# A longer hand-written order for the opening of a fused attention and feed-forward kernel

## Chip, cores and metric

The kernel runs on one core of a Trainium2 chip. The metric is device time in microseconds: the median of a few executions of the whole program. Executions taken for the trace are listed apart, and all views below are of one such execution.

## What is computed

Attention of 4 batches, 8 heads, 768 positions and 64 dimensions, in which each query sees the keys less than 16 positions away and, besides, 24 summary keys (the maximum over blocks of 32 keys) with summary values (the mean over the same blocks). Its output, 3072 rows of 512, goes through a feed-forward layer of 2048 hidden units with a soft gate:

```
k_sum = k.reshape(B, H, nb, block, D).max(axis=3)
v_sum = v.reshape(B, H, nb, block, D).mean(axis=3)
a = softmax([where(|i-j| < 16, scale * q k^T, -1e9), scale * q k_sum^T + log(32)])
x = a @ [v, v_sum]                      # -> (3072, 512)
h = x @ w_in                            # (512, 2048)
g = where(h >= 1, h, where(h <= -1, 0, (h + 1) ** 2 / 4))
out = g @ w_out                         # (2048, 512)
```

All data are float32; the two weight matrices reach the chip as 64-bit words and are turned into float32 there.

## The kernel before

**Tiling.** The rows are cut into 8 chunks of 384 (`c` = 0 to 7, two chunks a batch). A chunk's attention runs in 4 head couples (`p` = 0 to 3, two heads each). The hidden units are cut into 16 blocks of 128 (`f` = 0 to f, written in hexadecimal). The weights come in 16 tiles (`i` = 0 to f): tile i with i even holds blocks i and i+1 of `w_in`, tile i with i odd holds blocks i-1 and i of `w_out`.

**Steps.** Every piece of work is a step with a letter and its indices. Those that matter here, with their engine:

- SyncE (its queue issues all transfers): `r` raw keys of a couple (line 209), `y` raw values (228), `k`, `q`, `v` windows (215, 220, 235), `w` a weight tile (116, 119), `m` the mask (452), `g` the identity (465), `o` a result (448).
- TensorE: `S` scores (300), `T` transposes (344), `Z` transpose of the summary values (273), `A` values (358), `F` one of four pieces of a hidden block, three matmuls (395), `B` a hidden block into the output, nine matmuls (436).
- VectorE: `R` key maxima (248), `Y` value sums (256), `M` mask and row maxima (311, 315), `D` reciprocals (335), `c` six pieces a weight tile (150, 153, 165), `I` the gate's minimum (413), `L` the low part of x (381).
- ScalarE: `E` exponentials (326), `i` guard of the sums (331), `a`, `b` the first two conversions of a weight tile (132, 142), `G`, `H`, `J` of the gate (401, 407, 418), `V` the means (279), `P` and `X` evictions (351, 376), `U` an output tile out of the accumulators (444, the middle one on VectorE at 442).
- GpSimd: `K` key windows of the first chunk, `C` summary keys into the key tile (251), `N` normalisation (339), `W` summary values into the value tile (284), `d` and `e` the two halves of a weight tile (174, 186), `O` the low part of the gate (423).

So a head couple runs S, M, E, i, D, N, T, P, A, X, L, and needs C before S, and Z, V, W before A. A hidden block runs F, G, H, I, J, O, B. A weight tile runs w, a and b, c, d, e.

**What sets the order.** The string `OPENING` lists steps; `do(OPENING)` issues them under `tc.manual_schedule()`, in which every engine takes its instructions in the order of the list. It holds all of chunk 0, all weights, and the attention of chunk 1 with its first two hidden blocks. Behind it, from line 525 on, loops issue the rest under a manual order for TensorE alone; for the other engines a planner sorts the instructions, and it may also put one of these ahead of an instruction of the list. A step that stands in `done` is not issued twice. In the loop, hidden blocks come in pairs; at f = 2, 6, 10, 14 `turn` transposes a couple of the next chunk and issues the loads and sums of the couple after it (`r`, `k`, `q`, `R`, `C`), and at f = 0, 4, 8, 12 `meet` issues `A`, `X`, `L` of that couple and then `S` of the next one.

**Buffers.** The tag `w` of the pool `stage` has three buffers (`W_BUFS = 3`). They hold the raw keys `r` and values `y` of later batches, a weight tile between `c` and `e`, and the output tiles from `U` to the end of their store `o`. `ps` has six PSUM buffers, the hidden blocks two of their own.

**Small lists.** `P_DVE` and `X_DVE` name evictions that VectorE makes in place of ScalarE; `HI_POOL` names the weight tiles whose `d` GpSimd makes, the others being ScalarE's.

Of the kernel before, what the change touches and what calls it, by code (L numbers as in the profile page):

```python
# [38 lines left out]
LAG = 2  # L39
E_BUFS = 2  # L40
OPENING = """
r00 R00 K00 C00 q00 r01 R01 S00 m h M00 E001 E000 K01 g C01 q01 r03 i00 w0 y00 r02 K03 S01 b0 a0 R03 q02 M01 D00
N001 T001 P001 Y00 R02 Z00 E011 E010 N000 C03 T000 P000 i01 K02 C02 S02 c01 c00 c02 c04 c03 V00 w4 v00 b4 W00 q03
D01 y02 a4 M02 c05 N011 N010 d0 e0 E021 E020 y01 w2 c40 Y02 y03 v01 k10 v02 w1 A00 T010 P010 Y01 c42 c44 T011 P011
i02 X00 D02 S03 L00 M03 q10 N020 N021 b2 n Z01 V01 Z02 a2 V02 F010 T021 T020 Y03 Z03 W01 C10 c20 E030 F000 V03 W02
E031 c41 c21 A01 i03 c22 c23 v03 D03 N031 P021 P020 X01 k11 k12 v10 c24 A02 S10 N030 q12 q11 c43 c25 L01 T031 t d2
b1 T030 F001 w3 a1 X02 P030 P031 W03 M10 E101 A03 F011 X03 C11 e2 L02 c10 c45 C12 E100 i10 L03 F002 F012 F003 F013
w6 d4 G00 G01 H00 c11 c12 S11 D10 N101 S12 w8 w5 c14 c13 N100 I00 H01 T101 W10 w7 c15 I01 J00 F020 q13 T100 d1 k13
v12 wa wb w9 wc q20 F021 b3 P100 F030 O00 P101 M11 k20 r20 M12 a3 c31 F022 e1 F031 c30 c33 c32 c34 c35 F023 A10 wd
we F032 B00 F033 J01 O01 a6 G02 E120 H02 b6 I02 G03 H03 B01 e4 c60 b5 a5 J02 I03 J03 F040 c62 F050 d3 e3 F041 F051  # L50
X10 O02 b8 c61 c63 c64 F042 c50 c65 F052 c52 c51 c54 a8 F043 B02 F053 G04 a7 O03 c53 c55 H04 d6 e6 G05 H05 B03 d5 e5
I04 c80 I05 F060 b7 c81 c82 J05 L10 c83 c84 J04 aa E121 c70 c85 c72 c71 ba F070 i12 a9 c74 c73 c75 D12 F061 F071 O04
F062 F072 F063 B04 O05 d8 e8 G06 F073 G07 H06 I06 H07 B05 I07 ca0 ca2 ca1 ca4 ca3 ca5 F080 F090 F081 d7 N121 N120
T120 F091 P120 J06 F082 F092 J07 b9 e7 O06 F083 F093 T121 W12 da E110 E111 i11 G08 O07 ac H08 c90 c92 P121 c94 c91
I08 B06 A12 ea B07 c93 bc D11 X12 G09 H09 c95 d9 J08 O08 e9 bb F0a0 cc1 ab I09 cc0 L12 cc2 F0b0 cc3 J09 cc4 cc5 cb0
cb1 F0a1 ae cb3 cb2 cb4 F0b1 F0a2 F0b2 F0a3 F0b3 B08 O09 N111 T111 B09 dc G0a H0a G0b H0b be ec C13 I0a cb5 J0a P111
I0b v13 ce0 ce1 ce2 ce4 ce3 ce5 db N110 J0b v11 wf F0d0 ad bd F0c0 O0a F0d1 bf F0c1 F0d2 eb S13 F0c2 F0d3 F0c3 R20
O0b B0a M13 G0d T110 G0c H0d I0d cd0 C20 de ee W13 B0b H0c E130 E131 i13 F0f0 cd1 I0c J0c cd2 cd3 cd4 cd5 F0e0 F0f1
F0e1 af D13 cf0 cf1 cf2 F0f2 F0e2 F0f3 F0e3 O0c W11 N131 P110 dd cf4 cf3 A11 T131 J0d G0e H0e ed B0c O0d N130 cf5
I0e F110 G0f J0e H0f T130 X11 B0d P131 P130 I0f O0e F100 L11 df ef A13 J0f F111 F101 B0e F102 O0f B0f F112 X13 L13  # L60
F103 F113 U01 U02 U00 o02 o00 o01
"""
FIRST = [[("k", 2), ("q", 2)], [("k", 3), ("q", 3)], [("kraw", 1), ("vraw", 1)], [("kraw", 2), ("vraw", 2)],
         [("kraw", 3), ("vraw", 3)], [("v", 2), ("v", 3)], [("q", 0), ("q", 1)]]
K_COPY = "gggg"
H_DVE = "".split()
P_DVE = "110 120 121 131".split()
X_DVE = "11 13".split()
X_POOL = "".split()
F_DVE = "".split()  # L70
A_POOL = "".split()
HALF = "".split()
MASK_PE = "".split()
LATE = []
HI_POOL = [0, 1, 2, 3, 4, 5, 6, 8, 9, 10, 14, 15]


@with_exitstack
def fused_kernel(ctx: ExitStack, tc: tile.TileContext, q2, kT, kwin, vT, vwin, w_in, w_out, mask, ident, out):
# [28 lines left out]
    def room(i, what, shape, dtype):  # L108

        return wpool.tile(shape, dtype, tag=f"w{i}", name=f"{what}{i}")  # L110
# [60 lines left out]
    def convert_high(i):  # L171
        halves[i] = room(i, "halves", [P, 2, 2 * DM], F32R)
        if i in HI_POOL:
            nc.gpsimd.tensor_copy(out=halves[i][:, 0], in_=converting[i].bitcast(F32))
# [171 lines left out]
    def turned(c, p, j):  # L346
        pts[c, p, j] = att.tile([P, T], F32, tag=f"pt{j}", name=f"pt{c}_{p}_{j}", bufs=1)
        if f"{c}{p}{j}" in P_DVE:
            nc.vector.tensor_copy(out=pts[c, p, j][:KA], in_=t_pss[c, p, j][:KA, :T])
# [18 lines left out]
    def high(c, p):  # L368
        hi = xpool.tile([P, T], F32R, tag=f"xhi{p}", name=f"xhi{c}_{p}")
        lo = xpool.tile([P, T], F32R, tag=f"xlo{p}", name=f"xlo{c}_{p}")  # L370
        if f"{c}{p}" in X_POOL:
            nc.gpsimd.tensor_copy(out=hi, in_=fulls[c, p])
        elif f"{c}{p}" in X_DVE:
            nc.vector.tensor_copy(out=hi, in_=o_pss[c, p][:, :T])
# [233 lines left out]
```

## Time and profile before

| | us |
|---|---|
| median of 3 executions | 643.02 (642.08 to 643.59) |
| the profiled execution, whole | 644.87 |
| its span, first to last instruction | 643.1 |
| TensorE busy in it | 620.2 |
| ScalarE busy | 356.4 |
| GpSimd busy | 267.2 |
| VectorE busy | 245.2 |

The views are read like this: a timeline row has the start, the length, the engine, the line and operation, the tile written and the tiles read, the shape, and the number of like instructions put together; in brackets stands how long the engine had been idle before it and what released it. A row of the stages has the busy time of each engine in a stretch, the mean clock granted to TensorE, and the share and rate of the transfers. PEld is TensorE's weight load, SPq is SyncE's queue.

### The profile page before, as it was taken

The page shows a single profiled execution, that of the slowest core. Times are in us where ns is not written, and L with a number is a line of the kernel's source. Part 1 is how long each engine was busy: PE and PEld are TensorE (multiplying, and loading weights), DVE is VectorE, ACT ScalarE, POOL GpSimd, SP SyncE. Part 2 cuts the span into 40 slices and gives each one's busy share as a digit, 9 for nine tenths or more (in the row PEclk, how much of TensorE's full clock was granted, in tenths as well). Part 3 has the DMA queues.
Part 4 walks back from the last instruction along what each step waited for, and adds up shares of the span by engine and source line. Part 5 has one row for each costly group of instructions (what it writes and reads, how often), then busy time and mean ns, then how long its engine had stood idle before and what let it go on. Part 6 is the DMA issues. An engine that isn't in the chain of part 4 may idle for free.

```text
span 643.1 us, 11595 instructions
## 1 busy us (share of the span) xinstructions
PE 620.2 (96%) x4426; PEld 551.0 (86%) x4426; DVE 245.2 (38%) x465; ACT 356.4 (55%) x953; POOL 267.2 (42%) x307
## 2 busy tenths in 40 slices
PE   3699999899999999999999999999999999999997
PEld 2488888698888998898898898899889889889996
DVE  6989996542224322242122522142222312221111
ACT  4889994645545544654555554564454455443332
POOL 4689998334234333233334332334432333322221
PEclk9889999999999999999999999999999999999999
DMA  9999721632215222250123521052222200000001
GB/s 334 412 358 414 272 97 50 226 116 73 73 53 194 71 73 73 73 194 27 48 73 131 187 73 48 26 195 73 73 73 71 74 29 19 2 23 28 1 1 49
DMA packets 28167, 72.04 MB, mean 112 GB/s; under 512 B 2800, under 2 KB 3056, under 8 KB 28112
## 3 DMA queue, kind: packets, MB, share of 16 engines
q1 hardware_dynamic: 28112, 71.30, 31.5%
q8 instruction: 35, 0.57, 0.4%
q14 instruction: 20, 0.16, 0.1%
HBM read 65.00 MB, written 6.29 MB: 111 GB/s over the span
## 4 chain that ended last, share of the span: by engine, by line
PE 93%; DMA 4%; ACT 1%; issue 1%; POOL 1%; DVE 0%; SPq 0%; POOLq 0%; DVEq 0%
PE h L395 41%; PE acc L436 41%; PE o_ps L358 4%; PE s_ps L300 3%; PE t_ps L344 3%; DMA v<-in_vwin 2%; DMA first<-in_q 1%; DMA first<-in_kT 1%; ACT e L326 0%; POOL e L339 0%; ACT o L444 0%; ACT t L401 0%; POOL glo L423 0%; DVE e L311 0%; POOL v L284 0%
## 5 line engine op out<-in xcount | busy, mean ns | idle before, releaser
L395 PE MATMUL h<-xhi,halves 128*128 128x384 f32 x1024 | 277.8, 340 | 1.0 <-DVE t L413 1.0
L436 PE MATMUL acc<-halves,ghi 128*128 128x512 f32 x768 | 237.4, 390 | 0.0
L423 POOL TENSOR_TENSOR glo<-t,ghi 128x384 fp32r<-128x384 f32 x128 | 129.3, 1013 | 197.4 <-PE acc L436 184.5
L395 PEld LDWEIGHTS h<-xhi,halves 128*128 128x128 f32 x1024 | 186.2, 188 | 7.9 <-issue 4.0
L395 PE MATMUL h<-xlo,halves 128*128 128x384 f32 x512 | 172.2, 336 | 0.0
L436 PEld LDWEIGHTS acc<-halves,ghi 128*128 128x128 f32 x768 | 144.3, 188 | 28.3
L413 DVE SCALAR_TENSOR_TENSOR t<-h,t 128x384 f32<-128x384 f32 x128 | 71.0, 556 | 214.7 <-ACT t L407 212.9
L436 PE MATMUL acc<-halves,glo 128*128 128x512 f32 x384 | 152.6, 397 | 0.0
L401 ACT ACTIVATE t<-h,small 128x384 f32<-128x384 f32 x128 | 73.2, 573 | 90.9 <-PE h L395 89.2
L326 ACT ACTIVATE e<-e,den 128x120 f32<-128x120 f32 x192 | 73.3, 384 | 56.3 <-DVE den L315 56.3
L395 PEld LDWEIGHTS h<-xlo,halves 128*128 128x128 f32 x512 | 96.4, 188 | 1.8 <-DVE xlo L381 0.2
L418 ACT CAST ghi<-t 128x384 fp32r<-128x384 f32 x128 | 65.0, 510 | 54.5 <-DVE t L413 35.9
L436 PEld LDWEIGHTS acc<-halves,glo 128*128 128x128 f32 x384 | 72.2, 188 | 12.9 <-POOL glo L423 0.2
L407 ACT ACTIVATE t<-t 128x384 f32<-128x384 f32 x128 | 66.5, 524 | 2.2
L339 POOL TENSOR_TENSOR e<-e,den 128x360 f32<-128x360 f32 x64 | 49.2, 788 | 44.0 <-DVE den L335 43.6
L284 POOL COPY v<-mean 24x768 f32<-24x768 f32 x30 | 24.6, 821 | 84.4 <-DMA v<-in_vwin 45.6
L381 DVE TENSOR_TENSOR xlo<-o_ps,xhi 128x384 fp32r<-128x384 f32 x32 | 17.7, 554 | 79.0 <-ACT xhi L376 78.8
L376 ACT CAST xhi<-o_ps 128x384 fp32r<-128x384 f32 x30 | 14.3, 477 | 57.2 <-PE o_ps L358 57.2
L186 POOL TENSOR_TENSOR halves<-w,halves 128x1024 fp32r<-128x1024 f32 x16 | 38.6, 2412 | 0.6
L358 PEld LDWEIGHTS o_ps<-pt,v 120*64 120x64 f32 x720 | 24.6, 143 | 13.6 <-issue 10.6
L326 ACT ACTIVATION_READ_ACCUMULATOR e<-e,den 128x1 f32 x192 | 36.0, 188 | 0.0
L344 PE MATMUL t_ps<-ident_sb,e 128*120 128x128 f32 x192 | 29.3, 286 | 4.2 <-POOL e L339 4.2
(61 smaller groups left out, 404.6 us busy)
## 6 DMA issues: line engine op xcount, KB each, us to landing
v<-in_vwin SPq DMA_DIRECT2D x29, 384.0 KB, 3.3
q<-in_q SPq DMA_DIRECT2D x28, 384.0 KB, 4.3
k<-in_kwin SPq DMA_DIRECT2D x28, 360.0 KB, 5.0
raw<-in_w_in SPq DMA_DIRECT2D x8, 1024.0 KB, 11.3
raw<-in_w_out SPq DMA_DIRECT2D x8, 1024.0 KB, 13.3
out<-o SPq DMA_DIRECT2D x24, 256.0 KB, 2.1
kraw<-in_kT SPq DMA_DIRECT2D x13, 384.0 KB, 3.6
vraw<-in_vT SPq DMA_DIRECT2D x13, 384.0 KB, 3.9
```

The source lines that it names most:

```text
L186: nc.gpsimd.tensor_tensor(out=lo, in0=converting[i].bitcast(F32), in1=hi.bitcast(F32), op=ALU.subtract)
L326: nc.scalar.activation(out=es[c, p, j][:, t, :], in_=s[:, t, :], func=AF.Exp, bias=nm[:, t:t + 1], scale=scale, accum_out=den[:, t:t + 1])
L339: nc.gpsimd.tensor_tensor(out=e, in0=e, in1=den.unsqueeze(2).broadcast_to([P, NT, KA]), op=ALU.mult)
L344: nc.tensor.transpose(t_pss[c, p, j][:KA, t * P:(t + 1) * P], es[c, p, j][:, t, :], ident_sb)
L358: nc.tensor.matmul(o_pss[c, p][j * D:(j + 1) * D, cols], v_ts[c, p][:KA, blk, j * D:(j + 1) * D], pts[c, p, j][:KA, cols], start=True, sto ...
L395: nc.tensor.matmul(hs[c, f][:, :T], w[:, k], x, start=(k == 0 and n == 0), stop=(k == NK - 1 and n == len(products) - 1))
L401: nc.scalar.activation(out=ts[c, f], in_=hs[c, f][:, :T], func=AF.Relu, bias=ones_half, scale=0.5)
L407: nc.scalar.square(out=ts[c, f], in_=ts[c, f])
L413: nc.vector.scalar_tensor_tensor(out=g, in0=hs[c, f][:, :T], scalar=1.0, in1=ts[c, f], op0=ALU.max, op1=ALU.min)
L418: nc.scalar.copy(out=hi, in_=ts[c, f])
L423: nc.gpsimd.tensor_tensor(out=lo, in0=ts[c, f], in1=hi.bitcast(F32), op=ALU.subtract)
L436: nc.tensor.matmul(acc[c][i], a[:, rows], w, start=(f == 0 and n == 0), stop=(f == NF - 1 and n == len(products) - 1))
```

## The change

The list of the opening is replaced. The new one has 592 steps, the old one 544; no step of the old list is missing. The 48 that are added were issued by the loops before: hidden blocks 2 and 3 of chunk 1 (`F120` to `F133`, their `G`, `H`, `I`, `J`, `O`), `B10` and `B11`, and the couple (2, 0) from `y20`, `v20` and `S20` to `T200`, `T201`, `P200`, `P201`, with `Z20`, `V20`, `W20`. The order of nearly all other steps is new as well. The mask goes ahead of all loads; the scores of three couples come before the first transposes; weight tile 0 is loaded after nine loads of keys, queries and values, where it was loaded after five; tile 4 is converted after 2 and 1, where it was second. The three small lists are exchanged too: `P_DVE` 120, 121, 131 go, 111, 130, 200 come; `X_DVE` 13 goes, 03 comes; `HI_POOL` 10 and 14 go, 11 and 12 come.

The diff, with the first and the last lines of the two lists:

```diff
 OPENING = """
-r00 R00 K00 C00 q00 r01 R01 S00 m h M00 E001 E000 K01 g C01 q01 r03 i00 w0 y00 r02 K03 S01 b0 a0 R03 q02 M01 D00
-N001 T001 P001 Y00 R02 Z00 E011 E010 N000 C03 T000 P000 i01 K02 C02 S02 c01 c00 c02 c04 c03 V00 w4 v00 b4 W00 q03
-D01 y02 a4 M02 c05 N011 N010 d0 e0 E021 E020 y01 w2 c40 Y02 y03 v01 k10 v02 w1 A00 T010 P010 Y01 c42 c44 T011 P011
...
-I0e F110 G0f J0e H0f T130 X11 B0d P131 P130 I0f O0e F100 L11 df ef A13 J0f F111 F101 B0e F102 O0f B0f F112 X13 L13
-F103 F113 U01 U02 U00 o02 o00 o01
+m r00 R00 h K00 C00 q00 r01 R01 S00 M00 q01 K01 C01 E001 E000 i00 y00 r02 q02 r03 S01 y02 g R02 M01 K02 C02 w0 E010
+E011 y01 D00 Y00 v00 K03 N001 Y02 R03 S02 N000 Z00 T001 V00 i01 Z02 V02 P001 b0 D01 C03 N011 q03 N010 T000 M02 v01
+w2 a0 Y01 P000 E021 T010 c00 c02 Z01 V01 W00 c04 A00 T011 W01 c01 E020 c03 X00 L00 c05 i02 D02 n P010 P011 S03 A01
+d0 N020 T020 y03 k10 q10 N021 w1 C10 T021 M03 Y03 S10 a2 b2 t X01 e0 c20 L01 E030 E031 P020 i03 P021 c22 c21 c24 D03
+N030 Z03 v02 F010 W02 M10 b1 a1 V03 E100 c23 k12 v03 N031 T030 c10 c11 c25 A02 T031 P030 W03 F011 F000 c13 P031 C12
+X02 L02 c12 E101 d2 e2 A03 w4 q12 w3 q13 F001 F002 k13 a4 i10 w6 w5 X03 w7 b4 c14 L03 D10 w8 c15 c40 c41 c42 I01 I00
...
+F0f3 cd1 B0b af I0e cd2 cd4 v11 F0c0 cd3 L12 E130 G0f i13 H0f T111 I0f cd5 C20 F0c1 N110 J0e T110 O0e W11 F0c2 F0d0
+D13 P111 bf F0c3 P110 cf0 cf2 dd G0c H0c I0c J0c F0d1 A11 X11 F0d2 F110 L11 F0d3 ed N131 T131 F111 O0c N130 W13 cf1
+G0d H0d I0d P131 B0c cf3 cf4 cf5 F100 F112 T130 P130 F101 J0d S20 A13 X13 L13 y20 M20 Y20 O0d F102 B0d F103 df ef
+B0e F113 G10 H10 J0f O0f I10 F130 G11 v20 B0f J10 H11 E201 I11 J11 Z20 F120 V20 F131 F121 E200 O10 F132 F122 F133
+B10 G13 i20 U02 D20 W20 O11 F123 N201 B11 H13 I13 J13 O13 N200 G12 H12 U01 I12 J12 T200 T201 U00 P201 O12 o00 o02
+P200 o01
 """
...
-P_DVE = "110 120 121 131".split()
-X_DVE = "11 13".split()
+P_DVE = "110 111 130 200".split()
+X_DVE = "03 11".split()
...
-HI_POOL = [0, 1, 2, 3, 4, 5, 6, 8, 9, 10, 14, 15]
+HI_POOL = [0, 1, 2, 3, 4, 5, 6, 8, 9, 11, 12, 15]
```

Nothing else differs; what is computed is the same. Behind the new list TensorE's next steps are `A20`, then `S21`, then hidden block 4 of chunk 1; behind the old one they were `S20`, hidden blocks 2 and 3, `Z20`, `T200`, `T201`, `B10`, `B11`, `A20`, `S21`.

More of the change, by code (lines that the diff above doesn't have):

```diff
@@ L41 @@
 OPENING = """
-r00 R00 K00 C00 q00 r01 R01 S00 m h M00 E001 E000 K01 g C01 q01 r03 i00 w0 y00 r02 K03 S01 b0 a0 R03 q02 M01 D00
-N001 T001 P001 Y00 R02 Z00 E011 E010 N000 C03 T000 P000 i01 K02 C02 S02 c01 c00 c02 c04 c03 V00 w4 v00 b4 W00 q03
-D01 y02 a4 M02 c05 N011 N010 d0 e0 E021 E020 y01 w2 c40 Y02 y03 v01 k10 v02 w1 A00 T010 P010 Y01 c42 c44 T011 P011
-i02 X00 D02 S03 L00 M03 q10 N020 N021 b2 n Z01 V01 Z02 a2 V02 F010 T021 T020 Y03 Z03 W01 C10 c20 E030 F000 V03 W02
-E031 c41 c21 A01 i03 c22 c23 v03 D03 N031 P021 P020 X01 k11 k12 v10 c24 A02 S10 N030 q12 q11 c43 c25 L01 T031 t d2
@@ L47 @@
[L47 to L56, printed above, removed]
@@ L57 @@
-I0b v13 ce0 ce1 ce2 ce4 ce3 ce5 db N110 J0b v11 wf F0d0 ad bd F0c0 O0a F0d1 bf F0c1 F0d2 eb S13 F0c2 F0d3 F0c3 R20
-O0b B0a M13 G0d T110 G0c H0d I0d cd0 C20 de ee W13 B0b H0c E130 E131 i13 F0f0 cd1 I0c J0c cd2 cd3 cd4 cd5 F0e0 F0f1
-F0e1 af D13 cf0 cf1 cf2 F0f2 F0e2 F0f3 F0e3 O0c W11 N131 P110 dd cf4 cf3 A11 T131 J0d G0e H0e ed B0c O0d N130 cf5
-I0e F110 G0f J0e H0f T130 X11 B0d P131 P130 I0f O0e F100 L11 df ef A13 J0f F111 F101 B0e F102 O0f B0f F112 X13 L13
-F103 F113 U01 U02 U00 o02 o00 o01
+m r00 R00 h K00 C00 q00 r01 R01 S00 M00 q01 K01 C01 E001 E000 i00 y00 r02 q02 r03 S01 y02 g R02 M01 K02 C02 w0 E010
@@ new lines @@
+E011 y01 D00 Y00 v00 K03 N001 Y02 R03 S02 N000 Z00 T001 V00 i01 Z02 V02 P001 b0 D01 C03 N011 q03 N010 T000 M02 v01
+w2 a0 Y01 P000 E021 T010 c00 c02 Z01 V01 W00 c04 A00 T011 W01 c01 E020 c03 X00 L00 c05 i02 D02 n P010 P011 S03 A01
+d0 N020 T020 y03 k10 q10 N021 w1 C10 T021 M03 Y03 S10 a2 b2 t X01 e0 c20 L01 E030 E031 P020 i03 P021 c22 c21 c24 D03
+N030 Z03 v02 F010 W02 M10 b1 a1 V03 E100 c23 k12 v03 N031 T030 c10 c11 c25 A02 T031 P030 W03 F011 F000 c13 P031 C12
+X02 L02 c12 E101 d2 e2 A03 w4 q12 w3 q13 F001 F002 k13 a4 i10 w6 w5 X03 w7 b4 c14 L03 D10 w8 c15 c40 F012 F013 G01
@@ new lines @@
+c41 c42 F003 G00 v10 H01 I01 H00 I00 S12 c44 N101 N100 T101 T100 b3 d1 e1 c43 M12 J00 P101 J01 a3 O00 c30 c45 O01
+C13 F020 d4 e4 F030 F021 F031 F022 F032 F023 wa P100 we b6 G02 k11 w9 k20 B00 F033 H02 c32 B01 c31 c34 c33 a6 I02
+G03 H03 c35 I03 J02 b5 a5 F050 d3 O02 e3 F040 E120 J03 O03 c61 c60 c63 F051 F041 c62 c50 c64 E121 c52 c65 F052 F042
+F053 F043 G04 G05 H05 H04 c51 c54 c53 B02 S13 I05 i12 b8 a8 I04 d6 e6 c55 J04 B03 M13 J05 F070 c80 c81 c82 F060 c83
+b7 a7 c84 F071 F061 F072 d5 D12 v13 wd q20 c70 c85 O04 e5 F062 F073 ae aa O05 W10 d8 F063 G06 G07 c71 H07 ba B04 e8
@@ new lines @@
+A10 X10 H06 c72 c73 C11 c74 I07 c75 I06 a9 J06 B05 d7 F090 ca0 ca1 wf be ca2 b9 wb F080 ca3 ca4 L10 q11 ca5 F091 J07
+F081 c90 F092 F082 N120 O06 F093 F083 e7 c91 da B06 wc r20 O07 c92 G09 G08 H09 H08 ad N121 T121 B07 ea c93 c94 c95
+v12 I08 P121 d9 J08 O08 e9 I09 ce0 ce1 ce2 F0b0 J09 bb F0a0 F0b1 ab F0a1 ce3 ce4 ce5 T120 cb0 cb1 bd P120 F0a2 cb2
+cb3 cb4 cb5 F0b2 F0a3 F0b3 B08 W12 O09 de G0b G0a H0b H0a A12 ee I0a I0b S11 ac M11 J0b bc cc0 cc1 cc2 cc3 cc4 cc5
+E131 R20 B09 F0e0 F0f0 E111 F0e1 db O0b eb F0f1 F0e2 J0a O0a dc X12 F0f2 E110 i11 D11 N111 F0e3 cd0 ec G0e H0e B0a
```

## The prediction, made before the result was known

> **What bounds the kernel now.** I read the page's totals first, then the stages, then the timeline where a stage shows TensorE idle.
>
> ```profile
> span 643.1 us, 11595 instructions
> PE 620.2 (96%) x4426; PEld 551.0 (86%) x4426; DVE 245.2 (38%) x465; ACT 356.4 (55%) x953; POOL 267.2 (42%) x307
> ```
>
> ```profile
> 28.00:30.00 2.00, 0.57 (x11) 0.68 1.02 404
> ...
> 36.00:38.00 2.00, 1.82 (x29) 1.00 0.96 265
> ...
> 112.00:128.00 16.00, 13.12 (x87) 10.94 (x86) 7.82 (x14) 9.79 (x29) 4.62 (x6) 1.00 0.64 219
> ```
>
> TensorE is busy for 620.2 of 643.1 us. The change takes no work off it, so only its 22.9 idle us can move, and the time in which its granted clock is low. In the stages (stretch, TensorE busy, clock; the last row has all engines) the clock has fallen at 28 to 30 us and is 1.00 again from 36; after that, 112 to 128 stands out with 13.12 us busy of 16. Two places, then: the first 33 us, and the passage from the list to the loops. The opening, TensorE alone:
>
> ```profile
> 5.07 1.48 PE L300 MATMUL s_ps<-k,first 64*64 64x120 f32 x24 [5.07 <-POOL k L251]
> ...
> 13.47 0.89 PE L344 MATMUL t_ps<-ident_sb,e 128*120 128x128 f32 x3 [3.09 <-POOL e L339]
> ...
> 19.00 1.55 PE L358 MATMUL o_ps<-pt,v 120*64 120x64 f32 x24 [1.91 <-POOL v L284]
> ...
> 31.98 1.55 PE L358 MATMUL o_ps<-pt,first 120*64 120x64 f32 x24 [1.00 <-issue]
> ```
>
> The first scores, the first transposes and the first values wait for GpSimd. The last such gap ends at 31.98; from there TensorE has work up to the second place:
>
> ```profile
> 118.79 0.44 PE L395 MATMUL h<-xhi,halves 128*128 128x384 f32 x1 [1.03 <-DVE t L413]
> ...
> 124.40 0.27 PE L273 MATMUL vs_ps<-ident_sb,vsum 128*24 128x128 f32 x1 [1.05 <-DVE den L335]
> ...
> 125.28 0.54 PE L344 MATMUL t_ps<-ident_sb,e 128*120 128x128 f32 x3 [0.60 <-POOL e L339]
> ...
> 126.02 0.54 PE L344 MATMUL t_ps<-ident_sb,e 128*120 128x128 f32 x3 [0.20 <-POOL e L339]
> ...
> 130.61 0.92 PE L358 MATMUL o_ps<-pt,v 120*64 120x64 f32 x24
> 131.46 0.85 PE L300 MATMUL s_ps<-k,q 64*64 64x120 f32 x24
> ```
>
> Four gaps, 1.03 + 1.05 + 0.60 + 0.20 = 2.88 us: `S20` came just before, and between it and `T200` stood hidden blocks 2 and 3 alone, too little to cover mask, exponentials and normalisation. Here 130.61 is `A20` and 131.46 is `S21`. Everything that TensorE did before 131.46 it also does before `S21` in the new order, and behind `S21` both orders are alike, so **the change is worth the shift of `S21`**, and a lower clock behind it if TensorE has stood still.
>
> **First term: the gap at 118 to 126 goes, -2.88 us.** The new list has `S20` ahead of `A13`, three blocks `B0d` to `B0f`, hidden blocks 2 and 3 and `B10`, `B11`. The two blocks `B10`, `B11` alone took from 126.56 (126.02 + 0.54) to 130.61, 2.03 us each; five such blocks and the hidden ones more than cover what stood between `S20` and `T200`.
>
> **Second term: the opening.** VectorE and GpSimd turn the weights while TensorE waits, so I follow them to a place that both lists reach with the same work: the last piece of weight tile 3.
>
> ```profile
> 6.64 0.95 DVE L248 TENSOR_REDUCE ksum<-first 128x24 f32<-128x768 f32 x1 [2.00 <-DMA first<-in_kT]
> ...
> 27.52 1.88 DVE L150 TENSOR_SCALAR c<-raw 128x512 int32<-128x512 int32 x3 [0.47 <-ACT raw L132]
> ...
> 30.96 0.19 DVE L335 RECIPROCAL den<-den 128x6 f32<-128x6 f32 x1 [0.38 <-ACT den L331]
> ...
> 35.03 0.97 DVE L311 SCALAR_TENSOR_TENSOR e<-s_ps,mask_sb 128x360 f32<-128x360 f32 x2 [1.65 <-POOL first L284]
> 35.92 0.95 DVE L315 TENSOR_REDUCE den<-e 128x3 f32<-128x360 f32 x2
> ...
> 49.48 1.29 DVE L165 CUSTOM_DVE_ANT_0 w<-raw,c 128x1024 uint16<-128x1024 uint16 x2
> ```
>
> ```profile
> 21.62 2.37 POOL L186 TENSOR_TENSOR halves<-w,halves 128x1024 fp32r<-128x1024 f32 x1
> ...
> 50.84 1.04 POOL L174 CAST halves<-w 128x1024 fp32r<-128x1024 f32 x1
> 51.96 2.43 POOL L186 TENSOR_TENSOR halves<-w,halves 128x1024 fp32r<-128x1024 f32 x1
> ```
>
> ```profile
> L423 POOL TENSOR_TENSOR glo<-t,ghi 128x384 fp32r<-128x384 f32 x128 | 129.3, 1013 | 197.4 <-PE acc L436 184.5
> ```
>
> VectorE ended that piece at 50.77 (49.48 + 1.29). Up to it the new list has one mask step less (35.03 to 36.87, 1.84 us) and one eviction and one gate minimum more (the minimum takes 556 ns, the row of L413 below, and I take the eviction, of the same shape, as long): -0.73. The waits of 0.47, 0.38 and 1.65 us should go, since tile 2's conversions stand earlier on ScalarE and `S10` earlier on TensorE: -2.50. The wait of 2.00 us for the second raw keys stays and grows by about 0.4, my estimate for the mask that is now issued ahead of them. So the piece ends at 50.77 - 0.73 - 2.50 + 0.4 = 47.9. On GpSimd `d3` (1.04), `O02` (1.01) and `e3` (2.43, the row at 51.96, which ended at 54.39) follow: 52.4, 2.0 us earlier, while the piece on VectorE is 2.9 earlier. These tiles feed TensorE just in time, so **I take -2.4 us**, between the two. Bounds: 0, if TensorE runs dry at the start. Tile 0's second half ended at 23.99 (21.62 + 2.37), and in the new order it comes later: its load is behind four more loads, its pieces behind three more steps of VectorE, its split behind five more of GpSimd. The other end is -3.2, 0.73 and 2.50 with the mask for nothing.
>
> **Third term: what `S21` waits for now.** It needs summary keys, `C21`, these need `R21`, and this the raw keys `r21`, which lie in one of three buffers with the weight tiles and the output tiles.
>
> ```profile
> 102.74 7.15 SPq L235 DMA_DIRECT2D v<-in_vwin  x2
> ...
> 116.07 1.32 SPq L448 DMA_DIRECT2D out<-o  x3
> ...
> 118.83 0.37 SPq L209 DMA_DIRECT2D kraw<-in_kT  x1
> ...
> 124.28 0.33 SPq L209 DMA_DIRECT2D kraw<-in_kT  x1
> ...
> 127.34 0.95 DVE L248 TENSOR_REDUCE ksum<-kraw 128x24 f32<-128x768 f32 x1 [0.34 <-DMA kraw<-in_kT]
> ```
>
> ```profile
> 107.11 2.38 POOL L186 TENSOR_TENSOR halves<-w,halves 128x1024 fp32r<-128x1024 f32 x1
> ...
> 125.91 0.30 POOL L251 COPY k<-ksum 128x144 f32<-128x144 f32 x1
> ```
>
> From 109.49 (107.11 + 2.38), when the last weight tile was split, until the output evictions of 115 all three buffers were free; yet `r21` was issued only at 118.83, after the three stores. The planner did put later steps ahead of them: the second of the two loads at 102.74 is `v21`. So I read that buffers of a tag are given out in program order, first to the three output tiles of the list, then to `r21`. Before, that cost nothing: `C21` was through at 126.21, `S21` ran at 131.46.
>
> In the new list the stores stand as `o00 o02 o01`, and `U00` behind `J12` on ScalarE, which needs `F123`, the step ahead of `B11` on TensorE. Nothing of this depends on how early TensorE is free of chunk 0. The durations:
>
> ```profile
> L413 DVE SCALAR_TENSOR_TENSOR t<-h,t 128x384 f32<-128x384 f32 x128 | 71.0, 556 | 214.7 <-ACT t L407 212.9
> L401 ACT ACTIVATE t<-h,small 128x384 f32<-128x384 f32 x128 | 73.2, 573 | 90.9 <-PE h L395 89.2
> L418 ACT CAST ghi<-t 128x384 fp32r<-128x384 f32 x128 | 65.0, 510 | 54.5 <-DVE t L413 35.9
> L407 ACT ACTIVATE t<-t 128x384 f32<-128x384 f32 x128 | 66.5, 524 | 2.2
> ...
> out<-o SPq DMA_DIRECT2D x24, 256.0 KB, 2.1
> ```
>
> ```profile
> 125.86 0.48 ACT L351 COPY pt<-t_ps 120x384 f32<-120x384 f32 x1 [0.32 <-PE t_ps L344]
> ...
> 639.51 0.58 ACT L444 COPY o<-acc 128x512 f32<-128x512 f32 x1 [0.77 <-PE acc L436]
> ```
>
> - Without gaps the list's last transpose ends where `A20` began, less the two terms: 130.61 - 2.88 - 2.4 = 125.3. `B11` (2.03) and two transposes (about 1.0) lie behind `F123`, so that ends at 122.3.
> - ScalarE then still has `H13`, `J13` of the block before, about 0.5 us, then `G12` 0.57, `H12` 0.52, VectorE's `I12` 0.56, `J12` 0.51, `U00` 0.58: with hand-offs 125.6.
> - Store, 2.1: 127.7. `r21` until VectorE has it: 3.06, as from 124.28 to 127.34 for the next such load (others in flight can only lengthen it): 130.8. `R21` 0.95, `C21` 0.30: **`S21` at 132.1**.
> - TensorE is there earlier. `P201` (0.48) stands behind `U00` on ScalarE and ends at 126.1, so `A20` starts then and not at 125.3, +0.8. It takes 0.85 (130.61 to 131.46). `S21` could start at 127.0 and waits until 132.1, +5.1. Behind it all later work on TensorE stands in order, `F140` first.
>
> **Fourth term: the clock.** The row of 28 to 30 us shows it fall after gaps that leave 0.57 us of work in two; it was back by 36, some 3.6 us after the last gap ended at 31.98. The scores at 5.07 took 1.48 us, those at 131.46 0.85. I take 3.6 us at half speed behind `S21`, +1.8. Bounds: 0, since gaps of 2.88 in all within 8.3 us left 112 to 128 at 1.00; and 3.5, twice as long.
>
> **Sum**: -2.88 - 2.4 + 0.8 + 5.1 + 1.8 = +2.4 us. The profiled execution took 644.87 us, 1.8 more than its span and 1.85 more than the median of 643.02; both terms stand outside the change, so I add to the median: **645.4 us**.
>
> The Trainium skill, "TensorE: Matmul & The Clock Gate", section "Part 1: The HAM clock gate", has the clock fall after an idle window of about 3.4 us, with windows that run free. By that rule a gap of 5.1 us holds a whole window in half of the cases, (5.1 - 3.4) / 3.4; the trace's fall at 28 us came without one, as TensorE worked 0.57 us in that stretch.
>
> **The rivals.** Two per thousand, 1.3 us, is about what a measurement of this kernel can tell from no change.
>
> 1. *The forecast*, 645.4: 0.50.
> 2. *The wait without the clock*: the gap does not lower it, as the 2.88 us did not. 645.4 - 1.8 = 643.6. The Trainium skill's rule above is this case in half of its outcomes. For it speaks 112 to 128, against it 28 to 30. 0.20.
> 3. *`r21` is not late*, the other side: the planner gives it a buffer ahead of the output tiles, or `U00` runs early, and only the gap and the opening count. 643.02 - 2.88 - 2.4 + 0.8 = 638.5. It decides as soon as `r21` is issued before 122.0 (127.0 less 0.30, 0.95, 3.06 and hand-offs). Against it: `r21` at 118.83 behind `v21`. 0.15.
> 4. *The opening gains nothing*: tile 0 late, TensorE without work at about 28 us, the lead gone; the wait for `S21` moves with it. 645.4 + 2.4 = 647.8. For it: the wait of 5.07 and 3.09 us at the start stay, tile 0 is later; against it: VectorE's waits. 0.15.
>
> That it doesn't do what it says can hardly be: the list is taken literally.
>
> **How the numbers follow.** Faster by over 0.2%: the third case and some of the first, where the lead is 3.2 and the wait short: 0.22. Within 0.2%: mostly the second: 0.20. Slower: 0.58. The range, 640.0 to 649.0, runs from the forecast with lead 3.2, no fall of the clock and a shorter wait, past the fourth case with a clock low for 3.5; it leaves the third case out.
>
> **What would show it.** `S21` right after a wait of 3 to 6 us on GpSimd's summary keys, with `r21` issued two microseconds after `o00`: third term right. TensorE's clock below 1.00 near 132: fourth. `e3` ending near 52.4: second. No gap ahead of `Z20` and `T200`: first. A `r21` issued before the stores, or a first feed-forward matmul that leaves TensorE idle past 35 us, would make it wrong.

## The result, and the profile after

| | before | after |
|---|---|---|
| median | 642.55 us (641.73 to 643.59, 4 executions) | 649.58 us (648.52 to 650.08, 4 executions) |
| the profiled execution, whole | 644.87 | 650.08 |
| its span | 643.1 | 648.3 |

The ratio is 1.0106, with a 95% interval of 1.0085 to 1.0128: **slower by about 1%**, by more than the forecast and past the end of its range.

The totals of the page and its row of the clock, after:

```profile
PE 622.2 (96%) x4426; PEld 552.9 (85%) x4426; DVE 244.4 (38%) x465; ACT 356.5 (55%) x953; POOL 267.9 (41%) x307
...
PEclk9989999979999999999999999999999999999999
```

TensorE has the same 4426 instructions, 2.0 us more of busy time, and 26.1 us of idle time where it had 22.9. The clock is lowest in two slices, the third (32 to 49 us) and the ninth (130 to 146 us). The stages show where it fell: stretch, TensorE busy, its clock, share and rate of the transfers.

```profile
28.00:30.00 2.00, 1.05 (x4) 1.00 1.02 405
30.00:32.00 2.00, 1.19 (x9) 0.52 1.05 409
32.00:34.00 2.00, 2.00 (x28) 0.50 1.06 425
...
36.00:38.00 2.00, 2.00 (x29) 0.78 1.03 402
...
130.00:132.00 2.00, 0.00 (x0) 1.00 0.91 313
132.00:134.00 2.00, 0.00 (x0) 0.62 1.02 386
134.00:136.00 2.00, 1.51 (x25) 0.50 0.58 210
136.00:138.00 2.00, 2.00 (x7) 0.50 0.84 214
138.00:140.00 2.00, 2.00 (x10) 0.68 1.01 377
```

From 130 to 134 TensorE does nothing at all. Rows of the timeline of that place, all engines, in order of time (line numbers are two higher than before; the last row has 20 of the 24 matmuls of `S21`, which takes 1.48 us as a whole):

```profile
123.39 0.33 PE L397 MATMUL h<-xhi,halves 128*128 128x384 f32 x1
125.86 0.51 ACT L420 CAST ghi<-t 128x384 fp32r<-128x384 f32 x1 [0.69 <-DVE t L415]
126.02 0.87 PE L346 MATMUL t_ps<-ident_sb,e 128*120 128x128 f32 x6 [0.20 <-POOL e L341]
126.28 0.58 ACT L446 COPY o<-acc 128x512 f32<-128x512 f32 x1
126.88 1.33 SPq L450 DMA_DIRECT2D out<-o  x3
127.26 1.11 PE L360 MATMUL o_ps<-pt,v 120*64 120x64 f32 x24 [0.37 <-ACT o L446]
128.44 0.34 SPq L237 DMA_DIRECT2D v<-in_vwin  x1
128.91 0.38 SPq L211 DMA_DIRECT2D kraw<-in_kT  x1
129.60 0.33 SPq L230 DMA_DIRECT2D vraw<-in_vT  x1
130.39 0.33 SPq L211 DMA_DIRECT2D kraw<-in_kT  x1
133.11 0.95 DVE L250 TENSOR_REDUCE ksum<-kraw 128x24 f32<-128x768 f32 x1 [3.64 <-DMA kraw<-in_kT]
134.13 0.30 POOL L253 COPY k<-ksum 128x144 f32<-128x144 f32 x1 [6.69 <-DVE ksum L250]
134.49 1.28 PE L302 MATMUL s_ps<-k,q 64*64 64x120 f32 x20 [6.12 <-POOL k L253]
```

This is the chain that the forecast wrote down for its third term: last piece of `F123`, `J12`, `U00`, the stores, `r21` at 128.91, `R21`, `C21`, and `S21` at 134.49 behind a wait of 6.12 us. The gaps of before, at 118 to 126, are gone; 0.20 ahead of the transposes and 0.37 ahead of `A20` are left.

### The profile page after: what moved, and what is told of

Same layout as the page of the kernel before. It is cut to its first block, busy times and chain, and to the rows that moved or that the text cites. A ratio compares the mean times of both kernels' runs of the same rounds, so it can differ in the third digit from the quotient of the medians.

```text
span 648.3 us, 11601 instructions
## 1 busy us (share of the span) xinstructions
PE 622.2 (96%) x4426; PEld 552.9 (85%) x4426; DVE 244.4 (38%) x465; ACT 356.5 (55%) x953; POOL 267.9 (41%) x307
## 4 chain that ended last, share of the span: by engine, by line
PE 92%; ACT 3%; issue 2%; DVE 1%; DMA 1%; POOL 1%; SPq 0%; POOLq 0%; DVEq 0%; ACTq 0%
PE h L397 42%; PE acc L438 40%; PE o_ps L360 4%; PE s_ps L302 3%; PE t_ps L346 3%; ACT e L328 1%; DMA first<-in_kT 1%; ACT raw L144 0%; ACT pt L353 0%; POOL glo L425 0%; ACT raw L134 0%; DVE w L167 0%; DVE c L152 0%; ACT o L446 0%; DVE t L415 0%
## 5 line engine op out<-in xcount | busy, mean ns | idle before, releaser
L409 ACT ACTIVATE t<-t 128x384 f32<-128x384 f32 x128 | 66.7, 524 | 2.3
```

Of the source, the lines that this page charges most:

```text
L409: nc.scalar.square(out=ts[c, f], in_=ts[c, f])
```

## The experiments

Twelve runs were made, two of them repeats (before_again, u_again), each timed against the kernel before on the same chip. The theory behind them: `r21` waits for a store because of the order in which buffers are given out, and the wait costs more than its length, by the clock; the opening gains nothing where TensorE's clock behaves alike. Against it stand the forecast's second term (the opening gains 2.4 us) and the rivals of the prediction.

| label | what it is | median, us | to before, 95% |
|---|---|---|---|
| before_again | the kernel before | 642.98 | 0.9999 [0.9984, 1.0014] |
| o02_first | after, one store early | 644.53 | 1.0020 [1.0006, 1.0033] |
| u_early | after, all three evictions and stores early | 641.09 | 0.9971 [0.9953, 0.9990] |
| s21_later | after, `S21` two hidden blocks later | 646.01 | 1.0043 [1.0027, 1.0058] |
| warm_wait | after, idle transposes in the wait | 647.45 | 1.0071 [1.0048, 1.0093] |
| list_cut | after without the 48 steps | 646.47 | 1.0042 [1.0023, 1.0061] |
| warm_open | u_early, idle transposes in the opening | 638.84 | 0.9938 [0.9913, 0.9962] |
| warm_all | warm_open, more of them before 19 us | 638.99 | 0.9937 [0.9921, 0.9954] |
| old_plus | before with the 48 steps at its end | 646.46 | 1.0058 [1.0036, 1.0079] |
| old_plus2 | the same in another order | 647.46 | 1.0070 [1.0052, 1.0089] |
| old_open | u_early with the old list's first 43 us | 647.70 | 1.0084 [1.0065, 1.0103] |
| u_again | u_early, beside old_open | 640.71 | 0.9975 [0.9962, 0.9989] |

### Does `r21` wait for the stores?

One eviction's store is moved ahead (o02_first), or all three evictions and stores go to a place some eight microseconds earlier (u_early):

```diff
-B10 G13 i20 U02 D20 W20 ... T200 T201 U00 P201 O12 o00 o02 P200 o01
+B10 G13 i20 U02 o02 D20 W20 ... T200 T201 U00 P201 O12 o00 P200 o01
```

```diff
-... Z20 F120 V20 ... i20 U02 D20 ... H12 U01 I12 J12 T200 T201 U00 P201 O12 o00 o02 P200 o01
+... Z20 U02 U01 U00 o02 o01 o00 F120 V20 ... i20 D20 ... H12 I12 J12 T200 T201 P201 O12 P200
```

> The changed kernel with one store moved: o02 stands behind U02 in the list, ahead of o00 on SyncE's queue. Theory A (the loss is S21 waiting for r21, whose buffer is freed by the first store to end, plus the clock that falls in the wait): o02 issued near 122.5, r21 near 124.7 instead of 128.9, S21 near 130.2 instead of 134.5, wait of TensorE 1.9 us instead of 6.1, little or no fall of the clock: 4 to 6.5 us faster than the changed kernel, 643 to 645.5. Theory B (the buffer of r21 is a fixed one, that of U00): r21 stays at 128.9 and the time at 649.6. Theory C (the loss lies in the opening before 60 us): S21 earlier, but the time falls by under 2.

> The changed kernel with U02 U01 U00 and their stores moved up, from the list's end to behind Z20. Theory A: r21 is issued near 121 and C21 is through before TensorE comes to S21 at 128; no wait there, clock at 1.00: 6.1 us of wait and 2.2 us of clock gone, 641.3. Theory C (loss in the opening): 647 or more. Theory D (another wait takes the place, of the transposes of couple 1 or of the values): gap of 2 to 5 us between 128 and 150, 643.5 to 646.5.

The timeline of o02_first: store, `r21`, `S21`.

```profile
121.07 0.35 SPq L450 DMA_DIRECT2D out<-o  x1
123.12 0.33 SPq L211 DMA_DIRECT2D kraw<-in_kT  x1
...
129.31 1.12 PE L302 MATMUL s_ps<-k,q 64*64 64x120 f32 x24 [2.39 <-POOL k L253]
```

The first store to end sets `r21` free: it is issued two microseconds behind it, 5.8 us earlier than after, and `S21` waits 2.39 in place of 6.12 us. It is the store, and not merely a place behind it in the queue: `r21` is now ahead of the other two stores (125.43), and the queue stands 1.6 us at it until the store has ended (waits of SyncE's queue in o02_first, 118 to 126 us):

```profile
SPq L211 <- DMA out<-o: 1.6, 1, 1.6
```

In u_early:

```profile
118.75 1.65 SPq L450 DMA_DIRECT2D out<-o  x3
121.02 0.34 SPq L211 DMA_DIRECT2D kraw<-in_kT  x1
...
127.03 0.92 PE L360 MATMUL o_ps<-pt,v 120*64 120x64 f32 x24 [0.74 <-DVE pt L351]
127.88 0.85 PE L302 MATMUL s_ps<-k,q 64*64 64x120 f32 x24
```

`S21` follows `A20` without a wait, the clock stays at 1.00 there, and the kernel is 8.5 us faster than after (649.58 - 641.09). The reading of the buffers is right: they go to the output tiles first, whichever engine has time, and the price of the change as made is the place of six steps.

### What does the fall of the clock cost?

In s21_later `S21` stands behind hidden blocks 4 and 5 on TensorE; warm_wait has 45 transposes of the identity into an unused part of a hidden block's PSUM tile, between `A20` and `S21`. They add work that no result uses. First s21_later, then warm_wait (its new step `p`, the transposes, left out):

```diff
-                    meet(c, NPAIR - 1) if f == 0 else meet(c + 1, f // 4 - 1)
+                    if (c, f) == (1, 4):
+                        do("A20 X20 L20")
+                    else:
+                        meet(c, NPAIR - 1) if f == 0 else meet(c + 1, f // 4 - 1)
                 for n in (f, f + 1):
...
+                if (c, f) == (1, 4):
+                    meet(2, 0)
```

```diff
+                    if (c, f) == (1, 4):
+                        do("A20 X20 L20 p14f0 p14f1 p14f2")
                     meet(c, NPAIR - 1) if f == 0 else meet(c + 1, f // 4 - 1)
```

> The changed kernel with S21 put behind hidden blocks 4 and 5 of chunk 1 on TensorE (4.2 us of matmuls that need nothing of it); the list and r21's time as they are. Theory A: the wait ahead of S21 falls from 6.1 to about 1.9 us and the clock stays up: 4 to 6.4 us faster, 643.2 to 645.6. If the chain from S21 to T210 has become too short, a gap of 1 to 3 us ahead of T210: 645 to 647. Theory C: no more than 1 us gained.

> The changed kernel with 45 transposes of the identity (4.9 us) on TensorE between A20 and S21, into unused columns of the tile of hidden block 4; the results are not read. S21 still starts near 134.5, since r21 is as late. If the clock fell because TensorE stood still: 1.00 at 132 to 142, S21 in 0.85 instead of 1.48 us, 2 to 2.8 us faster than the changed kernel, 647.0 to 647.6. If it fell for another reason: 649.6.

Timeline and stages of warm_wait:

```profile
127.70 5.13 PE L405 MATMUL h<-ident_sb 128*128 128x128 f32 x45
...
134.02 0.85 PE L302 MATMUL s_ps<-k,q 64*64 64x120 f32 x24 [1.19 <-POOL k L253]
```

```profile
134.00:136.00 2.00, 1.98 (x31) 1.00 0.59 200
136.00:138.00 2.00, 2.00 (x13) 1.00 0.85 268
```

`S21` still waits for its keys, and starts at 134.02, but the clock holds. From there to the end of the span it is 511.7 us (645.7 - 134.02), as much as in before (643.1 - 131.46 = 511.6); after takes 513.8 (648.3 - 134.49). So **the low clock behind the wait costs 2.1 us**; the medians differ by as much (649.58 - 647.45). In s21_later hidden blocks 4 and 5 come between, and yet a wait of 3.34 us is left, in which the clock falls. The expectation (1.9 us of wait, 643.2 to 645.6 us) was missed at 646.01: `R21` stands on VectorE behind the gate's minimum of hidden block 5 and starts at 133.95 only, although its load was issued 0.7 us earlier than after.

```profile
135.31 1.48 PE L302 MATMUL s_ps<-k,q 64*64 64x120 f32 x24 [3.34 <-POOL k L253]
```

```profile
135.00:136.00 1.00, 0.69 (x16) 0.51 0.20 28
```

### What is the new opening worth?

list_cut is the new list without its 48 steps, the loops issuing these again as before, with `U02 U01 U00 o00 o02 o01` at its end. before_again is the unchanged kernel.

> The new opening alone: the new list without its 48 added steps, which the loops issue again, so U02, U01, U00 and the stores come straight behind B0f. If the new opening gains the 2.4 us of the prediction: 640.5. If it gains nothing against a common execution of before: 642.9. In both cases the four gaps of 2.9 us between S20 and T200 are back and S21 waits for nothing.

> The kernel before once more, for a second trace. If its opening is the same in every execution, span 643.1 and S21 at 131.5 again. If the profiled execution of before was a slow one (644.87 against a median of 642.55), S21 comes at 129 to 130.5, and TensorE's clock in the opening falls for a shorter time than from 28.7 to 35.6; ratio 1.000.

before_again showed what the first profile could not. Its clock is at 1.00 where that of the profiled execution of the prediction was 0.50 to 0.68, from 28 to 36 us; it is low for a shorter time and earlier, from 21.1 to 24.5:

```profile
24.00:26.00 2.00, 1.86 (x17) 0.87 1.03 410
...
28.00:30.00 2.00, 1.72 (x28) 1.00 1.03 413
...
34.00:36.00 2.00, 1.55 (x29) 1.00 1.02 386
```

Its span is 641.2 us, 1.9 less, as it was expected for the case that the first profile was of a slow opening. And the three waits of VectorE that the forecast wanted to remove, 0.47, 0.38 and 1.65 us, are not in it, though the order is the old one. The same three steps:

```profile
27.83 1.87 DVE L150 TENSOR_SCALAR c<-raw 128x512 int32<-128x512 int32 x3
...
30.80 0.18 DVE L335 RECIPROCAL den<-den 128x6 f32<-128x6 f32 x1
...
33.13 0.96 DVE L311 SCALAR_TENSOR_TENSOR e<-s_ps,mask_sb 128x360 f32<-128x360 f32 x2
```

The times of before lie between 641.6 and 645.2 us, and go with the clock. With a mean clock of 0.999 or 1.000 over the span the median is 642.2 us (26 of the 65 executions beside the experiments), with 0.996 or 0.997 it is 642.9 (19), below that 644.6 (20). The profiled execution of 644.87, at 0.995, is one of the last kind. For the new order every profile has a low clock in the opening but those of warm_open and warm_all, described below.

So like is to be set beside like. Ends of the last piece of tile 3 on VectorE, of `e3`, and of `e8` on GpSimd, in us; old_plus and old_plus2, also below, have the first 525 steps of the old list unchanged:

| | order | clock at half speed | tile 3 | `e3` | `e8` |
|---|---|---|---|---|---|
| before | old | 28.7 to 35.6 | 50.8 | 54.4 | 68.8 |
| before_again | old | 21.1 to 24.5 | 48.6 | 52.5 | 66.9 |
| old_plus | old | not low from 24 on | 48.4 | 52.3 | 66.7 |
| old_plus2 | old | not low from 24 on | 48.1 | 51.9 | 66.3 |
| after | new | 30.1 to 36.9 | 49.9 | 54.4 | 68.7 |
| u_early | new | 26.6 to 36.9 | 49.7 | 54.3 | 68.5 |
| s21_later | new | 25.8 to 36.0 | 49.1 | 53.6 | 67.9 |
| u_again | new | 31.8 to 35.2 | 49.2 | 53.7 | 68.0 |
| warm_wait | new | 31.7 to 35.1 | 49.2 | 53.7 | 68.1 |
| o02_first | new | 30.8 to 34.2 | 48.4 | 53.0 | 67.3 |
| list_cut | new | 27.1 to 30.5 | 47.9 | 52.4 | 66.7 |
| warm_open | new | not low from 24 on | 47.5 | 52.0 | 66.3 |
| warm_all | new | not low | 47.5 | 52.1 | 66.4 |

Where the clock is not low, two runs against two, the new opening leads by 0.6 to 0.9 us at tile 3, and at `e3` and `e8` the two orders lie within 0.4 us of each other, either way. Where it is low for the better part of 28 to 36 us (before against after and u_early), the lead is 0.9 to 1.1 at tile 3 and 0.0 to 0.2 behind it. With the clock behaving alike, nothing near the 2.4 us of the forecast is there. One warning on the clock's column: it reads 1.00 up to the first change on record, although the scores at 5 us take 1.48 us in all runs but warm_all, where they take 0.85.

list_cut is slower than before (646.47, where 640.5 or 642.9 was expected), for the same reason as after. Its timeline ahead of `Z20`:

```profile
116.30 1.92 SPq L451 DMA_DIRECT2D out<-o  x3
...
119.21 0.34 SPq L231 DMA_DIRECT2D vraw<-in_vT  x1
...
124.77 0.37 PE L276 MATMUL vs_ps<-ident_sb,vsum 128*24 128x128 f32 x1 [4.70 <-DVE vsum L259]
```

The raw values `y20` stand behind the stores in the buffers too: one gap of 4.70 us takes the place of the four of before. In before, too, VectorE stood 2.35 us for `y20`, issued behind the stores at 118.34, and the reciprocals for which `Z20` waits came right behind its sums. So a part of the gap of before was the stores' doing as well, where the prediction has it that the order of the buffers cost nothing before.

### What does the low clock in the opening cost?

warm_open is u_early with 17 idle transposes in TensorE's gaps between 24 and 31 us (the steps `p`); warm_all has 26 idle matmuls more, in the gaps before 19 us.

```diff
-d0 N020 T020 ...    N030 Z03 v02 ...    N031 T030 c10 c11 c25 A02
+d0 N020 p0180 T020 ...    N030 Z03 p0130 v02 ...    N031 p0021 T030 c10 c11 c25 p0040 A02
...
+    def warm(c, f, n, _):
...
+        for _ in range(n):
+            nc.tensor.transpose(hs[c, f][:, T:], ident_sb, ident_sb)
```

> The kernel u_early (new list, output tiles evicted early) with 17 transposes of the identity into unused columns of a hidden block's PSUM tile, where TensorE stood idle between 24 and 31 us; the results are not read. If the fallen clock at 26 to 37 us is what holds the opening back: clock 1.00 there, A03 near 34.5 instead of 36, VectorE's waits for X02 and X03 shorter, 639.0 to 640. If not: 641.1 as u_early, or slower by up to 1 us.

> The kernel warm_open with 26 more idle matmuls (128 x 128 of ones, results not read) in TensorE's gaps before 19 us. If the low clock of the first 24 us (24 score matmuls in 1.48 us) holds the opening back as well: scores in 0.85 us, c35 before 47, 637.5 to 638.5. If the loads and VectorE set the pace there: 638.8 as warm_open; if the idle matmuls get in the way of the scores: 639 to 641.

The stages of warm_open, as above:

```profile
28.00:30.00 2.00, 1.70 (x10) 1.00 1.02 405
...
32.00:34.00 2.00, 2.00 (x27) 1.00 1.06 426
```

The clock stays at 1.00 from then on, all four executions lie within 0.4 us (638.68 to 639.09), and the kernel is 2.25 us faster than u_early (2.0 if each is set against before on its own chip). It **beats both kernels**: 638.84 us, 0.62% under before. More idle work before 19 us (638.99) adds nothing, though it brings the first scores from 1.48 to 0.85 us.

### The old opening with the new passage

old_plus and old_plus2 keep the old opening and add the 48 steps in orders of my own; old_open takes the old list's order for the first 198 steps of u_early, up to `O01`, and that of u_early behind them (with `X03` on ScalarE, as in before).

> The old list with the 48 steps put in at its end: S20 ahead of A13, U01 U02 U00 and their stores where they were, hidden blocks 2 and 3, then T201, T200, B10, B11. If the passage alone is worth its 2.9 us and nothing takes their place: 640.0. If r21 is again late, a wait ahead of S21: 643 or more.

> The old opening with the passage of u_early: the old list up to the end of chunk 0, then S20 ahead of A13, output tiles evicted early, hidden blocks 2 and 3, B10, B11 and last T201, T200. If the two openings are worth the same when TensorE's clock behaves alike, the time is that of u_early, 641.1, within 1; u_early was measured 1.8 us below the kernel before, and its passage alone is 2.88 - 0.74 = 2.1 us better. If the new opening is the better one by the 2.4 us of the prediction: 643. If the new opening costs time: 639 to 640.

> The list of u_early with its first 198 steps (up to O01, about 43 us) in the order of the old list: old opening, same steps everywhere behind it, and the same order behind it. This is the second term alone. Theory A (the new order of the opening is worth nothing of its own; what differs is the clock that TensorE gets there): c35 of tile 3 ends within 0.7 us of that of u_early wherever the clock is alike; 641.1 us where the clock is low at 28 to 36 as in u_early, about 639.2 us, a little above the 638.84 of warm_open, where it stays at 1.00. Theory B, the forecast's second term (the new order is 2.4 us ahead): 643.5 us, e3 of tile 3 2.4 us later than in u_early.

> u_early once more, beside old_open on the same chip. Theory A: equal to old_open within 0.5 us, or up to 2.25 us slower where the low clock in the opening is in all of its executions and not in those of old_open. Theory B: 2.4 us faster than old_open.

None of the three gives the whole time that it was made for; the openings of old_plus and old_plus2 are the old order's at full clock, in the table above. In old_plus my tail had a gap of 4.05 us ahead of the transposes; in old_plus2 there was one of 3.47, since `G11` stood behind `E201`, `E200` and the evictions on ScalarE; the clock fell in both. In old_open the fault is at the seam. Its timeline, GpSimd, then TensorE:

```profile
50.36 0.30 POOL L254 COPY k<-ksum 128x144 f32<-128x144 f32 x1 [3.04 <-DMA k<-in_kwin]
...
54.16 0.44 PE L398 MATMUL h<-xhi,halves 128*128 128x384 f32 x1 [3.04 <-POOL halves L189]
```

The old order loads `k13` late, the new one has `C13` early: GpSimd stands 3.04 us for it, the halves of tile 4 queue behind it, and TensorE stands 3.04 us in turn. Both expectations missed: old_open is 7.0 us slower than u_again by medians, 5.2 by spans. Of the 5.2, 3.4 are idle time at that seam and 0.95 idle time before 46 us (16.66 against 15.71), with the clock low for 3.4 us in both; that last figure is all that the run says of the opening, and it lies between the theories. The rest of the 7.0 was not traced.

## Why the prediction was wrong in size

**First term, the gap at 118 to 126: right.** Of 2.88 us, 0.20 is left. The wait of `A20`, forecast at 0.8, is 0.37.

**Second term, the opening, -2.4: this step failed.** `e3` should have ended at 52.4 and ended at 54.43 in after (54.39 in before); the piece of tile 3 at 47.9 and ended at 49.90. What failed in it is the 2.50 us for three waits of VectorE that were to go. I took them for a property of the old order, and they came with the low clock of the one execution that I read: before_again, old_plus and old_plus2 have the old order and the clock at 1.00 from 28 to 36 us, and none of the three waits. The other item, 0.73 us less work, is near the 0.6 to 0.9 that tile 3 gains at full clock. With the low clock the new order has waits of its own. The timelines of after, VectorE and TensorE:

```profile
35.07 0.56 DVE L383 TENSOR_TENSOR xlo<-o_ps,xhi 128x384 fp32r<-128x384 f32 x1 [1.24 <-ACT xhi L378]
37.32 0.56 DVE L376 CAST xhi<-o_ps 128x384 fp32r<-128x384 f32 x1 [1.09 <-PE o_ps L360]
```

```profile
29.00 0.44 PE L397 MATMUL h<-xhi,halves 128*128 128x384 f32 x1 [0.74 <-POOL halves L188]
...
31.71 1.55 PE L360 MATMUL o_ps<-pt,first 120*64 120x64 f32 x24 [0.71 <-POOL first L286]
...
35.94 1.34 PE L360 MATMUL o_ps<-pt,first 120*64 120x64 f32 x24
```

These two steps of VectorE wait for values that TensorE works out at half clock: 1.55 us for what took 0.92 in before_again. In warm_open, with the clock held, 0.25 of the 1.24 is left and nothing of the 1.09. I had given the clock a term behind `S21` only.

The step from `e3` to TensorE failed as well: these tiles do not feed it just in time. TensorE is busy for 64.00 of the 64 us from 46 to 110 in before and in after, so an earlier `e3` starts nothing earlier. What the opening gains must show before 46 us. The start of `A20` less the gaps behind 46 us is 127.73 in before (130.61 - 2.88) and 126.69 in after (127.26 - 0.57): 1.0 us in place of 2.4, with the clock low for 6.8 us in both. So the rival of the opening that gains nothing (647.8, chance 0.15) is what happened at `e3`, while TensorE kept 1.0 of the 2.4; its other half, that the first feed-forward matmul would leave TensorE idle past 35 us, did not come (it ran at 29.00).

Whole times give a rough bound. At a mean clock of 0.999 or more before takes 642.2 us; u_early and u_again took 640.32 and 639.66 in one execution each, -1.9 and -2.5; warm_open takes 638.84, -3.4. The passage explains -2.1 (gaps of 2.81 in before_again, of 0.74 in u_early and warm_open). Between +0.2 and -1.3 is left for the opening.

**Third term, the wait for `S21`: right in kind, 1.0 too small.** Step by step, forecast and measured: `F123` ends at 122.3 and 123.72 (the opening's missing lead), `U00` at 125.6 and 126.86, `r21` is issued at 127.7 and 128.91, `R21` starts at 130.8 and 133.11. The load took 4.20 us where I had 3.06 from an unhurried one; `v21`, `r21`, `y21` and `r22` are now issued within two microseconds, right behind the stores. Whether these others lengthened it is not shown: in u_early, with `y21` and `r22` issued within 1.3 us of `r21`, it took 3.22 us. I had written that other transfers could only lengthen it and left it out of the sum.

**Fourth term, the clock: right**, +1.8 forecast and 2.1 measured; the clock stayed low for 4.8 us behind the start of `S21`, where I had taken 3.6. The rival of the wait without it (643.6) falls, and so does the one in which `r21` is not late (638.5): it was issued at 128.91.

**The sum.** `S21` came 3.03 us later than in the profiled execution of before (134.49 - 131.46) where +0.64 was forecast; with 2.1 to 2.2 for the clock that is 5.2, and the two profiled executions lie 5.2 apart (650.08 - 644.87). The rest is in the base: I put the sum on the median of 643.02 and took the 1.85 us by which the profiled execution lay above it as standing outside the change. It was the low clock in the opening, with the three waits that it brings. So the forecast took off the median, in part, a time that the profiled execution had and the median had not. So 649.58 - 645.4 = 4.2 is made up of 1.4 (the opening's lead at `F123`), 1.0 (`r21`), 0.3 (the clock) and about 1.4 (the base: 1.85 less 0.5 by which the profiled execution of after lies above its median). The upper end of the range was also short of its own words: the fourth case with a clock cost of 3.5 in place of 1.8 is 649.5, not 649.0.

What stays open: the exact size of the opening's order with everything behind it alike, as old_open broke at its seam. The runs bound it well short of the 2.4 us forecast.

## What to carry to other kernels

Where tiles of several purposes share a tag, read in which order the program asks for them: a load can stand behind a store that has nothing to do with it, and moving evictions and stores a few microseconds ahead (six steps here) was worth more than the whole new order. Before a difference is put on a median, look whether the profiled execution is a common one; here it lay 1.85 us above the median, with the clock low in one stretch. A wait seen in one profile need not belong to the order of the kernel: a second profile of the kernel before would have shown that three of the waits did not. When waits are taken off one engine, follow that engine to its next wait before counting the gain, and see whether the engine that bounds the kernel waits for it at all; and price the clock in every stretch where TensorE has gaps, not only in the one where a gap is added.

## What the runs showed of the hardware

**The clock fell after short gaps.** In o02_first TensorE's last work before the gap ended at 126.92 and `S21` began at 129.31:

```profile
129.00:130.00 1.00, 0.69 (x22) 0.87 1.01 396
130.00:131.00 1.00, 1.00 (x12) 0.50 1.05 316
...
133.00:134.00 1.00, 1.00 (x7) 0.92 0.78 310
```

After 2.39 us without work the clock fell, and it fell when `S21` was already running; it stayed at 0.50 for 3.4 us, from 129.7 to 133.1. In s21_later it fell at 135.1, after 3.1 us without work. The Trainium skill, "TensorE: Matmul & The Clock Gate", section "Part 1: The HAM clock gate", has it fall after an idle window of about 3.4 us; neither gap could hold one, so the measurement decides: a window need not be wholly idle. Its two steps, full and half, agree with the 1.00 and 0.50 of every low stretch here.

**Low stretches lasted one, two or three times 3.4 us**: 3.4 us (before_again, 21.1 to 24.5), 6.8 (before, 28.7 to 35.6) or 10.2 us (u_early, 26.6 to 36.9).

**Idle work pays.** 17 transposes whose results nobody reads, in gaps of 24 to 31 us, took 2.25 us off the kernel, and the executions, spread over 639.5 to 644.7 us in u_early, came within 0.4 us of each other.
